# The range checks of four steps, the start of a written row, three routing products and one weight split stand elsewhere

## The chip, the cores and the metric

The kernel runs on one core of one Trainium2 chip. The metric is device time in microseconds: from three runs of the kernel the median counts, and one further run was taken with the hardware profiler. TensorE does the matrix products, VectorE and ScalarE the elementwise work and the copies out of the matmul accumulators, GpSimd some of both, and SP issues most transfers.

## The reference

```python
def reference(**kwargs):
...
    attn_out = _attn_ref(**attn_kwargs)
    B, H, S, D = attn_out.shape
    x = np.ascontiguousarray(attn_out.transpose(0, 2, 1, 3)).reshape(B * S, H * D)
    x = _moe_ref(x=x, **moe_kwargs)
    return _moe2_ref(x=x, **moe2_kwargs)

def _attn_ref(q, k, v, a_re, a_im) -> np.ndarray:
    B, H, S, D = q.shape
    mag = np.sqrt(a_re * a_re + a_im * a_im)
    scale = np.minimum(mag, 0.999) / (mag + 1e-06)
    a_re_n, a_im_n = (a_re * scale, a_im * scale)
...
    for t in range(S):
        ar, ai = (a_re_n[:, :, t, :, None], a_im_n[:, :, t, :, None])
        new_re = ar * S_re - ai * S_im
        new_im = ar * S_im + ai * S_re
        kv = np.einsum('bhd,bhe->bhde', k[:, :, t], v[:, :, t])
        S_re, S_im = (new_re + kv, new_im)
        y[:, :, t] = np.einsum('bhd,bhde->bhe', q[:, :, t], S_re)
...
def _moe_ref(x, w_a, w_b, w_out) -> np.ndarray:
    a = x @ w_a
    b = x @ w_b
    return (a * b @ w_out).astype(np.float32)
...
def _moe2_ref(x, w_skip, w_gate, w1, w2) -> np.ndarray:
...
    do_compute = skip_score > 0
...
    e_idx = np.argmax(logits, axis=1)
...
        h = np.maximum(xc[mask] @ w1[e], 0.0)
        y[mask] = gate_w[mask, None] * (h @ w2[e])
    out[do_compute] = xc + y
    return out.astype(np.float32)
```

B, H, S, D are 4, 8, 768, 48; 3072 tokens of width 384, hidden 1536 in the gated layer, eight experts of hidden 1024. First a recurrence with complex decay, then a dense gated layer, then a layer that sends each token to one of eight experts.

## The kernel before

**Three stages run interleaved.** The recurrence is done in 24 units of 128 tokens (unit u belongs to chunk u div 4, batch u mod 4); two units make a pair. The gated layer is done in 12 groups g of 256 tokens, each fed by one pair, in 12 steps f over the hidden size (`moe1_step`). The expert layer follows at the end; its routing is worked out group by group while the gated layer runs.

**A step of the gated layer.** 18 matmuls (`ab{g}_{f}`, lines 647 to 649) make both hidden products of 128 columns, each weight and input split in a high and a low part. ScalarE copies one half out (`asb`), VectorE multiplies the other half onto it (line 655: the gated product), ScalarE mostly rounds the product (`gh`), VectorE or GpSimd takes the rest (`gl`, line 659), and two steps later six matmuls (`op{g}_0`, `op{g}_1`, lines 631 to 633) add the step to the group's output. Two accumulators serve `ab`, two `op`. The columns of w_gate and w_skip are folded into w_out (ten more columns, `w2s`; line 532 splits them), so a group's output holds the routing logits too. After the last step VectorE copies the logits (`lg`, line 670) and ScalarE the output (`xr`, line 674).

**A unit of the recurrence.** Exponent steps of VectorE and ScalarE (`t1`, `t2`, `lh`, `ll`) make the logs of the decays, two matmuls sum them along the tokens (`l2_{u}`; for the angles `tp_{u}`, fed by `tl` and `th`), sines and cosines turn q and k (`qr`, `kr`), TensorE transposes them, multiplies them in 32-row strips (line 461, into `pcs`), VectorE masks the product (`sc`, line 470), and 64 small matmuls make the output (`y{u}`, line 502) behind 48 that add to the state (`ds{u}`, line 412). `xt` (line 514) brings y into the form that the gated layer reads.

**Range checks.** A fast path is taken only where the decays lie in a range. For units 0 to 5 the test is late: `check_late` loads a_re again into a tile `chk` with one buffer, tests it (`least`, line 285), loads a_im into the same buffer and tests that (`largest`, line 288, into `immax`). The result is needed at the program's end only.

**Routing.** `pick` finds a group's best expert (`m`, `eq`, `rt_oh`, `rt_r`), TensorE counts places (`pp`, lines 735 to 737; while recurrence runs these products use the `pcs` accumulators), `place` makes slots (`sl`, line 789), TensorE makes the table's part (`pt`, line 803), and VectorE adds it to the table (`tbl`, line 804).

**What sets the order.** A scheduler orders each engine's instructions, but `keep_rows` ties some into written rows: `ORDER` for the program's start, `STEADY` for ScalarE and VectorE in the groups in between. In a row `gl{g}_2*3` means three writers of that tile and `:1` the second one; each is made to follow the one before it on its engine, without a wait. `PLACE` lists which of the weight splits and others go to which engine. In `att_trigs`, from a pair on whose first unit is `PORT` = 8 or more, both units' first steps are issued ahead of the rest.

Of the kernel before, what the change touches and what calls it, by code (L numbers as in the profile page):

```python
# [27 lines left out]
NG = 12  # L28
# [3 lines left out]
CAUSAL = 6  # L32
# [25 lines left out]
    "abs": {"scalar": (0, 1, 2, 3,)},  # L58
    "qs": {"gpsimd": (1, 5, 6, 7,)},
    "wh": {"gpsimd": (0, 4, 5,)},  # L60
    "wl": {"vector": (1, 4,)},
    "gl": {"gpsimd": (0, 1, 3, 4, 5, 9, 12, 13, 16, 17, 18, 20, 21,)},
    "add": {"gpsimd": (3,)},
    "magic": {"scalar": (2, 3,)},
# [14 lines left out]
ENGINES = {getattr(mybir.EngineType, x) for x in ("PE", "Activation", "DVE", "Pool")}  # L79
GF = 5  # L80
PORT = 8
ROWS = 64
WO = DM + 10
SKIP_IDX = 8192.0
# [1 line left out]
ORDER = {  # L86
# [5 lines left out]
}  # L92
# [1 line left out]

STEADY = {
    "Activation": "t1_{u}:2 t2_{u}:4 t1_{v}:2 t2_{v}:4 t4_{u}:0 t4_{v}:0 asb{g}_0 th{u} xr{p}*2 gh{g}_0 th{v} asb{g}_1 gh{g}_1 asb{g}_2 gh{g}_2",
    "DVE": "q{u} k{u} q{v} k{v} t4_{u} asb{g}_0 lg{p}*2 tl{u} t4_{v} gl{g}_0 tl{v} asb{g}_1 t3_{u}*2 gl{g}_1 t4_{u} asb{g}_2 qr{u}:1 kr{u}:1 gl{g}_2 t3_{v}*2 qr{u}:0 kr{u}:0 asb{g}_3 t4_{v} gl{g}_3 kr{v}:1 asb{g}_4 kr{v}:0 gl{g}_4 qr{v}:1 qr{v}:0 asb{g}_5 gl{g}_5 sc{u}_0 sc{u}_1 xt{n} asb{g}_6 gl{g}_6 t1_{x} t1_{y} asb{g}_7 t1_{x} ll{x} gl{g}_7 t1_{y} ll{y} asb{g}_8 gl{g}_8 sc{v}_0 sc{v}_1 im{x} imp{x} im{y} imp{y} xt{n} asb{g}_9 gl{g}_9 re{a} re{b} asb{g}_10 gl{g}_10 asb{g}_11 gl{g}_11",
}


def keep_rows(nc, after):

    writers = {}
    for i in nc.all_instructions():
        for o in list(i.outs)[:1]:
            t = getattr(getattr(o, "bass_ap", None), "tensor", None)
            if t is not None:  # L110
                writers.setdefault((i.engine, re.sub(r"_\d+$", "", t.name)), []).append(i)
        if type(i).__name__ == "InstLoadActFuncSet":
            writers.setdefault((i.engine, "tab"), []).append(i)
    for engine, words in ORDER.items():
        chain(writers, after, engine, words.split())
    for engine, words in STEADY.items():
        row = []
        for g in range(3, NG - 1):
            row += words.format(p=g - 1, g=g, n=g + 1, u=2 * g + 2, v=2 * g + 3, x=2 * g + 4, y=2 * g + 5, a=2 * g + 6, b=2 * g + 7).split()
        chain(writers, after, engine, row)  # L120


def chain(writers, after, engine, words):
# [12 lines left out]
def kern(tc, q, k, v, a_re, a_im, w_a, w_b, w_out, w_skip, w_gate, w1, w2, out):  # L136
# [3 lines left out]
    with st:  # L140
# [68 lines left out]
        def after(later, earlier, how=mybir.DependencyClass.NoSync):  # L209
            tc.add_manual_dep(  # L210
                later, earlier.name,
                mybir.DependencyInfo(how, mybir.DependencyReason.DATA),
                reason="table order",
            )
# [72 lines left out]
        def largest(i, im):  # L287
            return dve.tensor_reduce(out=immax[:, i : i + 1], in_=im, axis=AX.X, op=ALU.max, apply_absolute_value=True)

        def check_late(i):  # L290
            c, b = units[i]
            for src, test in ((a_re, least), (a_im, largest)):
                t = ew.tile([P, W], F32, tag="chk", name=f"chk{i}", bufs=1)
                ld = sync.dma_start(t.rearrange("t (h d) -> t h d", d=D), src[b, :, c * P : (c + 1) * P, :].rearrange("h t d -> t h d"))
                after(ld.ins, marks["ts", i + 6])
                test(i, t)

        def att_exp(i):
            c, b = units[i]
# [295 lines left out]
        def att_trigs(p):  # L595
            table("trig_and_small")
            steps = [att_trig(i) for i in (2 * p, 2 * p + 1)]
            if 2 * p >= PORT:
                for x in steps:
                    next(x)  # L600
            for x in steps:
                for _ in x:
                    pass
            if p == 0 and WARM:

                wm = bank("op", "warm", 2)
                for x in range(WARM):
                    pe.matmul(wm[:, :DM], ident, U[0]["ts"], start=True, stop=True)
            for i in (2 * p, 2 * p + 1):
                att_pe(i)  # L610
                if i >= CAUSAL and i % 2 == 0:
                    ready = sorted(picked)
                    for r in sorted(lgs):
                        pick(r, env.masked, env.pc[1])
                elif i > CAUSAL:
                    for r in ready:
                        place(r, env.masked, env.pc[0])
# [21 lines left out]
        def moe1_step(g, f):  # L639
            xt = M[g][0]  # L640
            fs = slice((f % 2) * P, (f % 2 + 1) * P)
            ab = bank("ab", f"ab{g}_{f}", 2)
            for x, nm in enumerate("ab"):
                o = ab[:, x * 256 : (x + 1) * 256]
                for c in range(NCC):
                    wh, wl = (env.w[nm, f // 2][:, y, c, fs] for y in range(2))
                    pe.matmul(o, wl, xt[:, c, 0], start=c == 0, stop=False)  # L647
                    pe.matmul(o, wh, xt[:, c, 1], start=False, stop=False)  # L648
                    pe.matmul(o, wh, xt[:, c, 0], start=False, stop=c == NCC - 1)  # L649
            if len(pend) == 2:  # L650
                moe1_out(*pend.pop(0))
            asb = env.mp.tile([P, 256], F32, tag="asb", name=f"asb{g}_{f}")
            n = NF * g + f
            copy(on("asb", n, act), asb, ab[:, :256])
            dve.tensor_tensor(out=asb, in0=ab[:, 256:], in1=asb, op=ALU.mult)  # L655
            gh = env.mp.tile([P, 256], F32R, tag="gh", name=f"gh{g}_{f}", bufs=3)
            copy(on("gh", n, act), gh, asb)
            gl = env.mp.tile([P, 256], F32R, tag="gl", name=f"gl{g}_{f}", bufs=3)
            on("gl", n).tensor_tensor(out=gl, in0=asb, in1=gh, op=ALU.subtract)  # L659
            pend.append((g, f, gh, gl))  # L660
# [635 lines left out]
```

## Time and profile before

| | us |
|---|---|
| median of 3 runs (832.26 to 834.45) | 832.45 |
| the profiled run | 831.85 |
| its span | 830.0 |
| TensorE busy | 786.5 |
| VectorE busy | 550.4 |
| ScalarE busy | 453.0 |
| GpSimd busy | 167.6 |

The span is what the profile covers; 1.85 us of the run lie outside it. Busy times are sums over the span; an engine with a small sum can still hold TensorE at one place, which only the waits of that place show.

### The profile page before, as it was taken

Reading aid. Unit: us, or ns where it says so; the run is one execution under the profiler, and the core shown is the slowest. Engines: PE = TensorE matmul, PEld = TensorE weight load, DVE = VectorE, ACT = ScalarE, POOL = GpSimd, SP = SyncE. Lnnn points to the kernel's source line nnn. Section 1 sums busy time; section 2 is a strip of 40 time slices with the busy share of each in tenths; the row PEclk is TensorE's granted clock in tenths of the full one; section 3 lists DMA queues with packets and bytes.
Section 4 is the critical chain, followed back from the end, with each engine's and each line's share of the span. In section 5 each row is a group of like instructions: output and inputs, shape, how many; then the busy total and the mean of one; then the engine's idle time right before and its main releaser. Section 6 shows DMA issues by size and latency. Waiting matters only on the chain.

```text
span 830.0 us, 22382 instructions
## 1 busy us (share of the span) xinstructions
PE 786.5 (95%) x9115; PEld 754.2 (91%) x9115; DVE 550.4 (66%) x1417; ACT 453.0 (55%) x949; POOL 167.6 (20%) x196
## 2 busy tenths in 40 slices
PE   1899999999999999999999999999999999999995
PEld 0589899999989989999999999998999989999995
DVE  7999888685676857757676576746747347555541
ACT  6897655473546644566455565555535226555540
POOL 3131443410100000000000000000003026666650
PEclk9999999999999999999999999999999999999998
DMA  9995223251342432213222231120105049667500
GB/s 253 251 316 121 54 63 68 46 122 33 77 89 38 106 64 72 54 36 87 51 68 55 52 81 36 50 49 11 40 18 176 1 164 338 215 222 208 180 22 23
DMA packets 180960, 83.17 MB, mean 100 GB/s; under 512 B 152084, under 2 KB 168026, under 8 KB 180848
## 3 DMA queue, kind: packets, MB, share of 16 engines
q1 hardware_dynamic: 178800, 76.26, 35.7%
q0 software_dynamic: 2048, 5.40, 1.8%
q8 instruction: 73, 1.20, 0.6%
q14 instruction: 39, 0.32, 0.1%
HBM read 69.84 MB, written 12.61 MB: 99 GB/s over the span
## 4 chain that ended last, share of the span: by engine, by line
PE 80%; DVE 6%; DMA 6%; ACT 3%; issue 2%; POOL 1%; SPq 0%; POOLq 0%; DVEq 0%; ACTq 0%
PE ab L647 11%; PE ab L648 10%; PE ab L649 10%; PE op L632 5%; PE op L631 5%; PE op L633 5%; PE y L502 4%; PE eh L954 3%; PE eh L955 3%; PE eh L957 3%; PE eo L971 3%; PE eo L972 3%; PE eo L973 3%; DMA chk<-in_a_im_dram 2%; PE pcs L461 2%
## 5 line engine op out<-in xcount | busy, mean ns | idle before, releaser
L647 PE MATMUL ab<-xt,wa 128*128 128x256 f32 x432 | 124.4, 288 | 0.5 <-DVE asb L655 0.4
L647 PE MATMUL ab<-xt,wb 128*128 128x256 f32 x432 | 123.0, 285 | 0.1
L648 PE MATMUL ab<-xt,wb 128*128 128x256 f32 x432 | 122.5, 284 | 0.0
L649 PE MATMUL ab<-xt,wb 128*128 128x256 f32 x432 | 122.4, 283 | 0.0
L649 PE MATMUL ab<-xt,wa 128*128 128x256 f32 x432 | 121.7, 282 | 0.0
L648 PE MATMUL ab<-xt,wa 128*128 128x256 f32 x432 | 121.6, 281 | 0.0
L659 DVE TENSOR_TENSOR gl<-asb,gh 128x256 fp32r<-128x256 f32 x131 | 62.6, 478 | 64.0 <-ACT gh L279 63.9
L632 PE MATMUL op<-wo,gh 128*128 128x394 f32 x288 | 99.2, 344 | 1.7 <-POOL wo L532 1.7
L633 PE MATMUL op<-wo,gh 128*128 128x394 f32 x288 | 98.7, 343 | 0.0
L631 PE MATMUL op<-wo,gl 128*128 128x394 f32 x288 | 98.5, 346 | 0.0
L279 ACT ACTIVATE asb<-ab 128x256 f32<-128x256 f32 x139 | 52.5, 378 | 68.8 <-PE ab L649 65.2
L647 PEld LDWEIGHTS ab<-xt,wa 128*128 128x128 f32 x432 | 81.4, 188 | 2.4 <-ACT asb L279 0.7
L648 PEld LDWEIGHTS ab<-xt,wb 128*128 128x128 f32 x432 | 81.5, 189 | 1.1 <-issue 1.0
L655 DVE TENSOR_TENSOR asb<-ab,asb 128x256 f32<-128x256 f32 x144 | 60.0, 417 | 33.3 <-ACT asb L279 33.1
L647 PEld LDWEIGHTS ab<-xt,wb 128*128 128x128 f32 x432 | 81.4, 188 | 0.6 <-DVE wb L532 0.3
L649 PEld LDWEIGHTS ab<-xt,wb 128*128 128x128 f32 x432 | 81.3, 188 | 0.7 <-issue 0.6
L648 PEld LDWEIGHTS ab<-xt,wa 128*128 128x128 f32 x432 | 81.4, 188 | 0.5 <-DVE xt L514 0.2
L649 PEld LDWEIGHTS ab<-xt,wa 128*128 128x128 f32 x432 | 81.5, 189 | 0.3 <-issue 0.2
L922 POOL TENSOR_TENSOR wq<-stg,wq 128x768 fp32r<-128x768 f32 x32 | 59.5, 1861 | 95.7 <-DMA stg<-in_moe_w_dram 46.4
L279 ACT ACTIVATE gh<-asb 128x256 fp32r<-128x256 f32 x132 | 54.4, 413 | 36.3 <-DVE asb L655 36.1
L264 POOL MEMSET v<- 128x64 f32 x24 | 3.5, 150 | 339.0 <-PE y L502 246.3
L961 DVE SCALAR_TENSOR_TENSOR hl<-eh,hh 128x256 fp32r<-128x256 f32 x64 | 27.1, 424 | 52.9 <-ACT hh L960 52.8
(268 smaller groups left out, 2021.2 us busy)
## 6 DMA issues: line engine op xcount, KB each, us to landing
stg<-in_moe_w_dram SPq DMA_DIRECT2D x28, 768.0 KB
rawa<-in_moe_w_a_dram SPq DMA_DIRECT2D x6, 768.0 KB
re<-in_a_re_dram SPq DMA_DIRECT2D x24, 192.0 KB
rawb<-in_moe_w_b_dram SPq DMA_DIRECT2D x6, 768.0 KB
q<-in_q_dram SPq DMA_DIRECT2D x24, 192.0 KB
k<-in_k_dram SPq DMA_DIRECT2D x24, 192.0 KB
rawo<-in_moe_w_out_dram SPq DMA_DIRECT2D x6, 768.0 KB
xd<-xr SPq DMA_DIRECT2D x24, 192.0 KB
```

Of the source, the lines that this page charges most:

```text
L279: return act.activation(out=out, in_=in_, func=AF.Copy) if e is act else e.tensor_copy(out, in_)
L502: ins = pe.matmul(o, l[:, col : col + STRIP], r, start=begin, stop=end).ins
L631: pe.matmul(o, gl[:, ts], wh, start=f == 0, stop=False)
L632: pe.matmul(o, gh[:, ts], wl, start=False, stop=False)
L633: i = pe.matmul(o, gh[:, ts], wh, start=False, stop=f == NF - 1)
L647: pe.matmul(o, wl, xt[:, c, 0], start=c == 0, stop=False)
L648: pe.matmul(o, wh, xt[:, c, 1], start=False, stop=False)
L649: pe.matmul(o, wh, xt[:, c, 0], start=False, stop=c == NCC - 1)
L655: dve.tensor_tensor(out=asb, in0=ab[:, 256:], in1=asb, op=ALU.mult)
L659: on("gl", n).tensor_tensor(out=gl, in0=asb, in1=gh, op=ALU.subtract)
L922: lo.tensor_tensor(out=o[:, 1], in0=t, in1=o[:, 0], op=ALU.subtract)
L961: vm = dve.scalar_tensor_tensor(out=gl, in0=o, scalar=0.0, in1=gh, op0=ALU.max, op1=ALU.subtract)
```

## The change

1. `PLACE` gives the small low split of group 3 of w_out to VectorE instead of GpSimd, and VectorE's written start row has it between the two `kr` products of unit 3 (`kr3*2` becomes `kr3 wo3 kr3`).
2. The written rows `STEADY` begin with group 2 instead of 3. In VectorE's row the second unit's exponent step comes ahead of the first unit's `ll`, and the table's sum stands behind the second `xt`.
3. The late checks' tests, kept in a list, are made to follow the gated products of steps 1, 4, 7 and 10 in groups 2, 3 and 4.
4. A row for TensorE in group 11 puts the routing products `pp10`, `pt9` and `pt10` behind whole `ab` blocks.
5. `att_trigs` issues both first steps ahead from pair 3 (`CAUSAL` = 6) instead of pair 4.

```diff
-    "wl": {"vector": (1, 4,)},
+    "wl": {"vector": (1, 3, 4,)},
...
+TESTS = (1, 4, 7, 10)
...
 STEADY = {
...
-asb{g}_7 t1_{x} ll{x} gl{g}_7 t1_{y} ll{y} asb{g}_8
+asb{g}_7 t1_{x} t1_{y} ll{x} gl{g}_7 ll{y} asb{g}_8
...
-im{y} imp{y} xt{n} asb{g}_9
+im{y} imp{y} xt{n} tbl:{r} asb{g}_9
...
+LAST = "ab11_3*18 pp10*3 ab11_4*18 pt9*4 ab11_6*18 pt10*4 ab11_7"
...
-        for g in range(3, NG - 1):
+        for g in range(2, NG - 1):
...
+    chain(writers, after, "PE", LAST.split())
...
+        tests = []
+
         def check_late(i):
...
-                test(i, t)
+                tests.append(test(i, t).ins)
...
-            if 2 * p >= PORT:
+            if 2 * p >= CAUSAL:
                 for x in steps:
                     next(x)
...
-            dve.tensor_tensor(out=asb, in0=ab[:, 256:], in1=asb, op=ALU.mult)
+            i = dve.tensor_tensor(out=asb, in0=ab[:, 256:], in1=asb, op=ALU.mult).ins
+            if g >= 2 and f in TESTS and tests:
+                after(tests.pop(0), i)
```

The diff's two pieces of `STEADY` are cut from VectorE's row. The rows below show how the order of instructions moves; a tile's name ends in its unit or group and a running number, and the lines of the changed kernel are 5 to 9 higher.

VectorE in group 4, around the masked scores of unit 10 and the routing of group 3, before:

```order
L659 TENSOR_TENSOR gl4_5_4630<-asb4_5_4625,gh4_5_4628 128x256
L285 TENSOR_SCALAR chk5_4444,remin_88<-chk5_4444 128x384
L470 TENSOR_TENSOR sc10_0_4171<-pcs0_2188,keep_86 128x512
L470 TENSOR_TENSOR sc10_1_4189<-pcs1_2189,keep_86 128x512
L713 TENSOR_REDUCE m3_4254<-lg3_3958 128x2
L288 TENSOR_REDUCE immax_87<-chk5_4447 128x1
L721 SCALAR_TENSOR_TENSOR eq3_4258<-lg3_3958,m3_4254,desc_117 128x8 x2
L723 TENSOR_TENSOR dl3_4261<-lg3_3958,m3_4254 128x16
L725 TENSOR_REDUCE m23_4263<-eq3_4258 128x2
L728 SCALAR_TENSOR_TENSOR rt_oh_132<-eq3_4258,m23_4263,sk3_4256 128x8 x2
```

The same place after, and the two places where the tests now stand:

```order
L668 TENSOR_TENSOR gl4_5_4630<-asb4_5_4625,gh4_5_4628 128x256
L477 TENSOR_TENSOR sc10_0_4171<-pcs0_2188,keep_86 128x512
L477 TENSOR_TENSOR sc10_1_4189<-pcs1_2189,keep_86 128x512
L722 TENSOR_REDUCE m3_4254<-lg3_3958 128x2
L730 SCALAR_TENSOR_TENSOR eq3_4258<-lg3_3958,m3_4254,desc_117 128x8 x2
...
L662 TENSOR_TENSOR asb4_7_4689<-ab4_7_4664,asb4_7_4689 128x256
L290 TENSOR_SCALAR chk5_4444,remin_88<-chk5_4444 128x384
...
L662 TENSOR_TENSOR asb4_10_4785<-ab4_10_4760,asb4_10_4785 128x256
L293 TENSOR_REDUCE immax_87<-chk5_4447 128x1
```

Both tests of unit 5 left the stretch between `gl4_5` and the routing's one-hot.

TensorE at the start of group 2, around the last `op` of group 1 (`op1`, fed by `gl1_11`), before:

```order
L648 MATMUL ab2_2_2725<-xt2_1657,wb1_491 128x256
L631 MATMUL op1_0_1381<-wo5_1275,gl1_11_2124 128x394
L632 MATMUL op1_0_1381<-wo5_1275,gh1_11_2122 128x394
...
L632 MATMUL op1_1_1382<-wo5_1275,gh1_11_2122 128x394
L633 MATMUL op1_1_1382<-wo5_1275,gh1_11_2122 128x394
L649 MATMUL ab2_2_2725<-xt2_1657,wb1_491 128x256
```

After:

```order
L656 MATMUL ab2_2_2725<-xt2_1657,wb1_491 128x256
L638 MATMUL op1_0_1381<-wo5_1275,gl1_11_2124 128x394
...
L640 MATMUL op1_1_1382<-wo5_1275,gh1_11_2122 128x394
L276 MATMUL tp_6_2288<-tl6_2290,tri_r_74 128x384
L277 MATMUL tp_6_2288<-th6_2289,tri_r_74 128x384
L638 MATMUL op2_0_2671<-wo0_507,gl2_0_2697 128x394
L639 MATMUL op2_0_2671<-wo0_507,gh2_0_2695 128x394
```

Before, the last matmul of `ab2_2` and the 18 of `ab2_3` follow `op1`, `tp_6` was inside `ab2_1` and `op2` came after `ab2_3`; now `tp_6` and `op2` follow `op1` directly.

TensorE and VectorE around the odd unit 13 in group 5, TensorE before and after:

```order
L412 MATMUL ds13_5230<-u13_5152,kr13_4987 32x48 x3
L502 MATMUL y13_5255<-tq13_5154,state1_91 32x128 x4
L648 MATMUL ab5_9_5593<-xt5_4249,wb4_1172 128x256
L649 MATMUL ab5_9_5593<-xt5_4249,wb4_1172 128x256
L647 MATMUL ab5_9_5593<-xt5_4249,wb4_1172 128x256
```

```order
L419 MATMUL ds13_5230<-u13_5152,kr13_4987 32x48 x3
L509 MATMUL y13_5255<-tq13_5154,state1_91 32x128 x4
L509 MATMUL y13_5255<-sc13_0_5210,v13_4051 32x128
L509 MATMUL y13_5255<-tq13_5154,state1_91 32x128
L509 MATMUL y13_5255<-sc13_0_5210,v13_4051 32x128 x2
```

VectorE before and after:

```order
L318 SCALAR_TENSOR_TENSOR t1_14_5712<-t1_14_5712,t2_14_5713 128x384
L327 TENSOR_TENSOR ll14_5726<-t1_14_5712,lh14_5725 128x384
L659 TENSOR_TENSOR gl5_7_5559<-asb5_7_5554,gh5_7_5557 128x256
L318 SCALAR_TENSOR_TENSOR t1_15_5741<-t1_15_5741,t2_15_5742 128x384
L327 TENSOR_TENSOR ll15_5755<-t1_15_5741,lh15_5754 128x384
L655 TENSOR_TENSOR asb5_8_5586<-ab5_8_5561,asb5_8_5586 128x256
L329 TENSOR_TENSOR imp14_4908<-imp14_4908,t2_15_5742 128x384
L659 TENSOR_TENSOR gl5_8_5591<-asb5_8_5586,gh5_8_5589 128x256
L470 TENSOR_TENSOR sc13_0_5210<-pcs0_2188,keep_86 128x512
```

```order
L325 SCALAR_TENSOR_TENSOR t1_14_5712<-t1_14_5712,t2_14_5713 128x384
L325 SCALAR_TENSOR_TENSOR t1_15_5741<-t1_15_5741,t2_15_5742 128x384
L334 TENSOR_TENSOR ll14_5726<-t1_14_5712,lh14_5725 128x384
L668 TENSOR_TENSOR gl5_7_5559<-asb5_7_5554,gh5_7_5557 128x256
L334 TENSOR_TENSOR ll15_5755<-t1_15_5741,lh15_5754 128x384
L662 TENSOR_TENSOR asb5_8_5586<-ab5_8_5561,asb5_8_5586 128x256
L336 TENSOR_TENSOR imp14_4908<-imp14_4908,t2_15_5742 128x384
L668 TENSOR_TENSOR gl5_8_5591<-asb5_8_5586,gh5_8_5589 128x256
L477 TENSOR_TENSOR sc13_0_5210<-pcs0_2188,keep_86 128x512
```

TensorE's whole `y13` (32 entries) now follows `ds13`, where before all but four entries stood behind `ab5_9` and `ab5_10`; on VectorE `t1_15` changed places with `ll14`.

## Rows read from the trace of the kernel before

**Rows 1.** The page: span and busy time of the engines.

```profile
span 830.0 us, 22382 instructions
PE 786.5 (95%) x9115; PEld 754.2 (91%) x9115; DVE 550.4 (66%) x1417; ACT 453.0 (55%) x949; POOL 167.6 (20%) x196
```

**Rows 2.** Windows: us of span; PE busy (instructions), PEld, DVE, ACT, POOL, clock, DMA, GB/s.

```profile
300.00:560.00 260.00, 259.81 (x3615) 250.77 (x3615) 174.81 (x510) 147.79 (x333) 10.37 (x20) 1.00 0.26 57
```

**Rows 3.** Timeline 88 to 92 (start, duration, instruction, [idle before, releaser]); tile wo (min/median/max ns).

```profile
91.41 0.45 PE L632 MATMUL op<-wo,gh 128*128 128x394 f32 x1 [1.67 <-POOL wo L532]
88.12 3.24 POOL L532 TENSOR_TENSOR wo<-w2s,wo 128x20 fp32r<-128x20 f32 x1 [4.22 <-ACT wo L279]
88.52 0.54 DVE L391 TENSOR_TENSOR kr<-k,ts 128x384 f32<-128x384 f32 x1
L532 POOL TENSOR_TENSOR wo<-w2s,wo x4: 230/256/3238, 55.1 to 115.8; 128x20 fp32r<-128x20 f32 x4
L532 DVE TENSOR_TENSOR wo<-w2s,wo x2: 167/167/167, 63.9 to 105.0; 128x20 fp32r<-128x20 f32 x2
```

**Rows 4.** Timeline, group 2, first recurrence unit (6): TensorE, SP's queue, VectorE.

```profile
187.02 0.30 PE L502 MATMUL y<-sc,v 128*32 128x128 f32 x1 [1.58 <-DVE sc L470]
180.99 0.37 SPq L294 DMA_DIRECT2D chk<-in_a_re_dram  x1
184.67 0.55 DVE L285 TENSOR_SCALAR_CACHE_REDUCE chk<-chk 128x384 f32<-128x384 f32 x1 [0.48 <-DMA chk<-in_a_re_dram]
```

**Rows 5.** Timeline, groups 3 and 4, the routing: TensorE and VectorE.

```profile
243.67 0.17 PE L735 MATMUL pcs<-rt_oh,ustrict 128*128 128x16 bf16 x1 [0.81 <-DVE rt_oh L728]
297.06 0.17 PE L735 MATMUL pcs<-rt_oh,ustrict 128*128 128x16 bf16 x1 [2.02 <-DVE rt_oh L728]
295.58 0.55 DVE L288 TENSOR_REDUCE immax<-chk 128x1 f32<-128x384 f32 x1 [1.87 <-DMA chk<-in_a_im_dram]
```

**Rows 6.** Timeline, start of group 5: first and last of six w_out matmuls, then VectorE.

```profile
326.52 0.35 PE L631 MATMUL op<-wo,gl 128*128 128x394 f32 x1
327.44 0.34 PE L633 MATMUL op<-wo,gh 128*128 128x394 f32 x1
327.99 0.54 DVE L362 SCALAR_TENSOR_TENSOR tl<-t,th 128x384 fp32r<-128x384 f32 x1
329.23 0.42 DVE L659 TENSOR_TENSOR gl<-asb,gh 128x256 fp32r<-128x256 f32 x1 [0.15 <-ACT gh L279]
```

**Rows 7.** Timeline, group 5: even unit (12), then odd unit (13).

```profile
344.99 1.29 DVE L470 TENSOR_TENSOR sc<-pcs,keep 128x512 int32<-128x512 int32 x2 [0.67 <-PE pcs L461]
345.27 0.26 PE L412 MATMUL ds<-v,kr 128*32 128x48 f32 x6
346.14 0.28 PE L502 MATMUL y<-sc,v 128*32 128x128 f32 x1
356.49 0.53 ACT L279 ACTIVATE lh<-t 128x384 fp32r<-128x384 f32 x1
357.05 0.56 DVE L327 TENSOR_TENSOR ll<-t,lh 128x384 fp32r<-128x384 f32 x1 [3.00 <-ACT lh L279]
359.41 0.56 DVE L327 TENSOR_TENSOR ll<-t,lh 128x384 fp32r<-128x384 f32 x1 [1.00 <-ACT lh L279]
359.73 0.26 PE L412 MATMUL ds<-v,kr 128*32 128x48 f32 x6
361.13 1.28 DVE L470 TENSOR_TENSOR sc<-pcs,keep 128x512 int32<-128x512 int32 x2
```

**Rows 8.** Timeline, groups 9 and 11: TensorE's last waits, and VectorE's wait ahead of one.

```profile
565.90 0.35 PE L647 MATMUL ab<-xt,wa 128*128 128x256 f32 x1 [0.42 <-DVE asb L655]
571.97 0.25 DVE L804 TENSOR_TENSOR tbl<-tbl,pcs 128x96 f32<-128x96 f32 x1 [1.57 <-PE pcs L803]
572.83 0.42 PE L271 MATMUL l<-ll,tri_r 128*128 128x384 f32 x1 [0.91 <-DVE xt L514]
641.29 0.20 PE L803 MATMUL pt<-rt_r,sl 128*128 128x48 bf16 x1 [1.21 <-DVE sl L789]
```

More of the change, by code (lines that the diff above doesn't have):

```diff
@@ L96 @@
     "Activation": "t1_{u}:2 t2_{u}:4 t1_{v}:2 t2_{v}:4 t4_{u}:0 t4_{v}:0 asb{g}_0 th{u} xr{p}*2 gh{g}_0 th{v} asb{g}_1 gh{g}_1 asb{g}_2 gh{g}_2",
-    "DVE": "q{u} k{u} q{v} k{v} t4_{u} asb{g}_0 lg{p}*2 tl{u} t4_{v} gl{g}_0 tl{v} asb{g}_1 t3_{u}*2 gl{g}_1 t4_{u} asb{g}_2 qr{u}:1 kr{u}:1 gl{g}_2 t3_{v}*2 qr{u}:0 kr{u}:0 asb{g}_3 t4_{v} gl{g}_3 kr{v}:1 asb{g}_4 kr{v}:0 gl{g}_4 qr{v}:1 qr{v}:0 asb{g}_5 gl{g}_5 sc{u}_0 sc{u}_1 xt{n} asb{g}_6 gl{g}_6 t1_{x} t1_{y} asb{g}_7 t1_{x} ll{x} gl{g}_7 t1_{y} ll{y} asb{g}_8 gl{g}_8 sc{v}_0 sc{v}_1 im{x} imp{x} im{y} imp{y} xt{n} asb{g}_9 gl{g}_9 re{a} re{b} asb{g}_10 gl{g}_10 asb{g}_11 gl{g}_11",
+    "DVE": "q{u} k{u} q{v} k{v} t4_{u} asb{g}_0 lg{p}*2 tl{u} t4_{v} gl{g}_0 tl{v} asb{g}_1 t3_{u}*2 gl{g}_1 t4_{u} asb{g}_2 qr{u}:1 kr{u}:1 gl{g}_2 t3_{v}*2 qr{u}:0 kr{u}:0 asb{g}_3 t4_{v} gl{g}_3 kr{v}:1 asb{g}_4 kr{v}:0 gl{g}_4 qr{v}:1 qr{v}:0 asb{g}_5 gl{g}_5 sc{u}_0 sc{u}_1 xt{n} asb{g}_6 gl{g}_6 t1_{x} t1_{y} asb{g}_7 t1_{x} t1_{y} ll{x} gl{g}_7 ll{y} asb{g}_8 gl{g}_8 sc{v}_0 sc{v}_1 im{x} imp{x} im{y} imp{y} xt{n} tbl:{r} asb{g}_9 gl{g}_9 re{a} re{b} asb{g}_10 gl{g}_10 asb{g}_11 gl{g}_11",
 }
+LAST = "ab11_3*18 pp10*3 ab11_4*18 pt9*4 ab11_6*18 pt10*4 ab11_7"
 def keep_rows(nc, after):
@@ L117, in keep_rows @@
         row = []
-        for g in range(3, NG - 1):
-            row += words.format(p=g - 1, g=g, n=g + 1, u=2 * g + 2, v=2 * g + 3, x=2 * g + 4, y=2 * g + 5, a=2 * g + 6, b=2 * g + 7).split()
+        for g in range(2, NG - 1):
+            row += words.format(p=g - 1, r=g - 2 if g > 2 else 9 * NG, g=g, n=g + 1, u=2 * g + 2, v=2 * g + 3, x=2 * g + 4, y=2 * g + 5, a=2 * g + 6, b=2 * g + 7).split()
         chain(writers, after, engine, row)
+    chain(writers, after, "PE", LAST.split())
 def chain(writers, after, engine, words):
```

2 rows, old and new, of the table ORDER are left out of this document.

## Prediction

> **What bounds the kernel now.** I read the page's totals first, then TensorE's busy time in windows, then its waits, then the timeline around each wait. TensorE is busy 786.5 of 830.0 us [rows 1]: the kernel is bound by TensorE, and an edit pays only by what it takes from the 43.5 us in which TensorE stands still. The windows tell where those are not: from 300 to 560 us TensorE is busy 259.81 of 260.00 us at a granted clock of 1.00 [rows 2]. So groups 5 to 8 have nothing to give, and the start (before 60 us) and the routed stage (after 680 us) are not touched by the change. What lies between and can be touched is seven single waits: 1.67 us for a small split of the w_out weights [rows 3], 1.58 us for the masked scores `sc` of unit 6 in group 2 [rows 4], 0.81 and 2.02 us for the routing's one-hot in groups 3 and 4 [rows 5], and 0.42, 0.91 and 1.21 us late in groups 9 and 11 [rows 8]. Behind each stands a VectorE or GpSimd instruction that was late in its own queue.
>
> **The change part by part.** The profiled run is 831.85 us, its span 830.0, and the other 1.85 us lie outside the span; I make the sum against 831.85.
>
> *The small split of group 3 of w_out.* GpSimd's split lasts from 88.12 to 91.36, and TensorE resumes at 91.41 after 1.67 us [rows 3]. The other splits of that form on GpSimd take 0.23 to 0.26, two on VectorE 0.17. On VectorE it stands between two `kr` products; the second began at 88.52, so the split ends near 88.7, a full microsecond before TensorE came to need it (91.41 - 1.67 = 89.74). Gain 1.67; the 0.17 more on VectorE falls on `kr`, whose transpose stands behind this block of `op` in TensorE's order. The row shows a GpSimd instruction that is twelve times as long as its equals while VectorE runs without a pause beside it. The Trainium skill (SBUF — State Buffer, section "Who interferes with whom") says that a VectorE instruction with two SBUF inputs and a GpSimd instruction that reads SBUF exclude each other, whichever issues first holding on; the stretched split agrees with that. By that rule the length is GpSimd's loss of the port and goes away with the move; if it were the cost of this instruction's data, VectorE would pay 3.24 us from 88.5, and the term would be a loss of some 0.4 us. The 0.17 us of VectorE's own splits is the row nearest to the moved one.
>
> *The written row begins with group 2.* TensorE waited 1.58 us for `sc` of unit 6, which VectorE reached late because a range check and the next pair's exponent steps stood ahead of it; the check itself began at 184.67 after 0.48 us for its load [rows 4]. In the changed order no exponent step stands there, unit 0's two checks stand behind the products of steps 3 and 4 and so over a step earlier, and TensorE arrives later besides: 1.58 gained. But the same row takes a cover away. Before, one matmul of ab2_2, then ab2_3, stand between group 1's last `op` and the next `tp`. Now `tp_6` and group 2's first `op` follow group 1's last `op` at once, while VectorE's row demands that group 1's logits be copied before `tl6`, and ScalarE's that `xr1` be copied before `gh2_0`. What this chain lasts is to be read in group 5, which has the same row: the six `op` of a step start from 326.52 to 327.44, 0.18 apart; `tl` ends at 328.53, `gl` at 329.65 [rows 6]. There a step's `ab` matmuls cover it. Without the cover TensorE would wait from 327.62 to about 329.72, less 0.36 us for the two `tp` at the same pace: a new wait of 1.75 us in two pieces. Bounds 1.0 (only the `tl` piece, 328.6 - 327.62) and 2.3 (a further `tl` of 0.54 between). I take 1.75. Group 2 alone thus pays nothing: 1.58 - 1.75.
>
> *The four range checks behind gated products.* In groups 3 and 4 the check of the imaginary part stood between the routing's maximum and its one-hot, and waited for its load (1.87 us in group 4); TensorE's routing product waited 0.81 and 2.02 [rows 5]. Now they stand behind the products of steps 7 and 10, where nothing that TensorE soon needs is queued right behind: `gl` of that step, used two steps later. What follows in the old place is the one-hot itself: without the check it can end 2.3 us earlier in group 4 (1.87, and 0.47 that the check holds VectorE), more than the 2.02; I take group 3 to go the same way. Gain 2.83 in full. Each check costs VectorE 0.55 us as before. The loads share one buffer, so the second load leaves when the first check is done; three steps lie between, against 3.7 us that such a load took (issued 180.99, its check at 184.67) [rows 4]; `ds` of units 12 and 13, three steps apart, lie 14.5 us apart [rows 7]. The loads stand in SP's queue ahead of `re10` and `re11`, needed a group later. The other two checks of group 3 and of group 4, tied to steps 1 and 4, keep the places that they had behind those, with waits on VectorE for which TensorE did not wait before; bounds for what that may do now 0 and 0.55, one check's length, taken as 0.
>
> *Odd units.* With the new row TensorE's `y` of the odd units 9 to 19 follows `ds` at once; before, most of `y` stood behind some 20 `ab` and `op` matmuls. An even unit already runs so: `sc` begins at 344.99, 0.28 us before `ds`, and `y` takes it at 346.14 with no wait. The odd one's `sc` began at 361.13, 1.40 us after `ds` at 359.73 [rows 7]: at that place `y` would wait 1.26 us. Does the row bring `sc` forward? VectorE's `ll15` began only at 359.41, on `lh15`, which ScalarE makes after `t1_15`; and VectorE had put `t1_15` behind `ll14` and its wait of 3.00 us for `lh14` (ScalarE, 356.49). Now `t1_15` comes ahead of `ll14`, and ScalarE makes `lh15` as second instruction after `lh14`, done near 358 at 0.53 apiece; `ll15` runs some 1.4 us sooner, and `sc`, then held by `gl5_8`, begins near 359.9. That is 0.17 after `ds` where the even unit has 0.28 before it, so up to 0.45 late; the even unit's `y` left some of that unused, since `sc`'s first half ended near 345.65 and was taken at 346.14. I take 0.2 for each of the six units: cost 1.2, bounds 0 and 2.7.
>
> *The rest.* In group 9 the gated product ahead of `sc` comes sooner (0.42), and `xt` now goes ahead of the table's sum, which itself waited 1.57 us [rows 8]: 0.25 of the 0.91, since its `y` is not earlier. In group 11 the routing product waits 1.21 us for its slots [rows 8]; two steps further on they are long there: 1.21. The product of group 0 now stands right behind `y6` with two groups' routing in front of it, which for one group takes 1.0 us from the end of the check to the product (296.05 to 297.06) [rows 5]; `y` itself covers most of a second one: cost 0.2, bounds 0 and 1.0.
>
> Sum: 1.67 + 1.58 + 2.83 + 0.42 + 0.25 + 1.21 = 7.96 gained; 1.75 + 1.2 + 0.2 = 3.15 lost; net 4.8 us. From 831.85 that is 827.05, from the median 832.45 it is 827.65; I say 827.3, as if the time before were 832.1.
>
> **The rivals.** *A, the odd units keep their late `sc`.* If ScalarE's row brings nothing forward, each of the six waits 1.26: 7.6 instead of 1.2, and 6.4 more make 833.7, no change. For it: ScalarE's `gh5_8` and `t2_15` are still ahead of `sc`; against it: the order moves exactly the product that held `lh15`. *B, on the other side, the same place worse.* ScalarE's row now puts `asb5_8` behind `lh15`. If `t1_15` comes no sooner than now, `lh15` still ends near 359.4, and `asb5_8`, its product, `gh5_8` and `gl5_8` come one after another behind it, 0.4 to 0.55 each: `sc` near 361.5, 1.77 after `ds`, a wait of 1.64 per unit. Six times that is 9.8 instead of 1.2, 8.6 more: 835.9, slower. From 1.0 us a unit on all gains are gone (6.0 / 6), from 1.5 the kernel is slower. *C, nothing new appears.* If the covers hold in group 2 and the odd units, the gain is 8.0 less 0.2: 824.3. *D, the split and the late waits are gone but come back behind the next instruction:* TensorE arrives 1.67 us earlier at everything that follows in the start, where loads set the pace, and half of the 7.96 is given back: 831.3.
>
> **How the numbers follow.** A measurement can tell about 0.3% from no change, 2.5 us: 829.95 and 834.95 are the limits. My forecast 0.58 (825 to 829.95), C 0.12 (823.5 to 825), D 0.11 (829.95 to 831.5), A 0.11 (831.5 to 834.95), B 0.08. Faster: 0.58 + 0.12 = 0.70. Same: D and A, 0.22. Slower: B, 0.08. The range from 823.5 to 831.5 holds the forecast, C and D, 0.81.
>
> **What would show it.** In the changed profile: no wait on the split near 90 us; two pieces of about 1.0 and 0.75 us on `tl` and `gl` at the start of group 2, and none on `sc` of unit 6; no wait on the one-hot in groups 3 and 4; TensorE without a wait at the odd units' `y`, or with 0.2 us; none on the slots in group 11. Waits of over a microsecond at each odd unit would mean A or B, and a new wait between 92 and 160 us D. The prediction is wrong if group 2's new wait is far from 1.75, or if TensorE's busy time itself moves.

## The result

The changed kernel takes 825.62 us in the median of four runs (825.35 to 825.83), the kernel before 833.16 beside it (832.26 to 834.45): a ratio of 0.9908, with an interval from 0.9891 to 0.9925. It is faster by 7.5 us; 827.3 and a gain of 4.8 were forecast, and the time lies inside the range. The two profiled runs differ by less, 831.85 against 825.83, 6.0 us. Where the rest comes from is told below, with the clock.

The page of the changed kernel, its span and totals:

```profile
span 824.1 us, 22362 instructions
PE 784.9 (95%) x9115; PEld 754.1 (92%) x9115; DVE 549.9 (67%) x1418; ACT 452.4 (55%) x949; POOL 164.0 (20%) x195
```

Against [rows 1] the span is 5.9 us shorter; TensorE's busy time fell by 1.6, its idle time from 43.5 to 39.2. TensorE's waits of the changed kernel (line, what was waited for: us in total, times, longest), with the large ones of the start left out:

```profile
PE op L638 <- DVE gl L668: 1.8, 2, 1.6
PE eh L963 <- DVE hl L970: 1.1, 1, 1.1
PE pg L825 <- DVE rt_r L788: 1.0, 1, 1.0
PE ab L654 <- DVE asb L662: 1.0, 2, 0.7
PE y L509 <- issue: 0.9, 3, 0.4
PE tp L276 <- DVE tl L369: 0.7, 1, 0.7
...
PE l L276 <- DVE xt L521: 0.6, 1, 0.6
```

The split, the scores of unit 6, both one-hots, the slots of group 11 and the 0.42 us of group 9 ([rows 3, 4, 5, 8]) are gone from it, and 0.91 at `l` became 0.6. A wait on a gather in the routed stage, `PE xgp L938 <- DMA xg<-xd,giu: 0.7` before, is gone too; no term stood for it. It goes with the row's start: it is 0.6 to 0.8 in all six kernels here whose written row begins with group 3, and at most 0.2 in the seven whose row begins with group 2; why isn't shown. New are two waits at the start of group 2 and two in group 3. TensorE's timeline there:

```profile
170.11 0.44 PE L276 MATMUL tp<-tl,tri_r 128*128 128x384 f32 x1 [0.72 <-DVE tl L369]
170.97 0.45 PE L638 MATMUL op<-wo,gl 128*128 128x394 f32 x1 [0.24 <-DVE gl L668]
261.53 0.38 PE L654 MATMUL ab<-xt,wa 128*128 128x256 f32 x1 [0.68 <-DVE asb L662]
265.51 0.45 PE L638 MATMUL op<-wo,gl 128*128 128x394 f32 x1 [1.60 <-DVE gl L668]
```

The first two are the pair that was forecast (1.0 and 0.75), at 0.96 us together. The chain behind them, the last `op` on TensorE and the logits, the output and `gl` on VectorE and ScalarE:

```profile
168.88 0.17 DVE L679 COPY lg<-op 128x10 f32<-128x10 f32 x1 [2.90 <-PE op L640]
169.04 0.34 PE L640 MATMUL op<-wo,gh 128*128 128x394 f32 x1
169.09 1.03 ACT L683 ACTIVATE xr<-op 128x384 f32<-128x384 f32 x2 [4.22 <-DVE lg L679]
170.51 0.40 DVE L668 TENSOR_TENSOR gl<-asb,gh 128x256 fp32r<-128x256 f32 x1
```

The last two waits, 2.28 us, no step had. VectorE's timeline in group 3 shows what they hang on:

```profile
260.89 0.25 DVE L813 TENSOR_TENSOR tbl<-tbl,pcs 128x96 f32<-128x96 f32 x1 [2.08 <-PE pcs L812]
261.06 0.42 DVE L662 TENSOR_TENSOR asb<-ab,asb 128x256 f32<-128x256 f32 x1
264.64 0.82 DVE L668 TENSOR_TENSOR gl<-asb,gh 128x256 fp32r<-128x256 f32 x1 [3.16 <-ACT gh L284]
```

In group 3 two groups' tables are summed (groups 0 and 1). The row now puts the second sum ahead of the gated product `asb3_9`, and TensorE makes its input only after `l2` of the next pair. VectorE waits 2.08 us with `asb3_9` behind it; and since `l2` is done by then, ScalarE goes into the next pair's exponents and a load of its function table before it gets to `gh3_9`:

```profile
260.43 1.64 ACT L235 ACTIVATE t<-l 128x384 f32<-128x384 f32 x4 [1.00 <-PE l L277]
262.07 1.28 ACT L208 ACT_TABLE_LOAD   x1
263.37 0.94 ACT L235 ACTIVATE t<-imp 128x384 f32<-128x384 f32 x2
264.21 0.40 ACT L284 ACTIVATE gh<-asb 128x256 fp32r<-128x256 f32 x1
```

At the odd unit 13 TensorE doesn't wait. VectorE and TensorE there, to be read against [rows 7]:

```profile
353.80 0.56 DVE L334 TENSOR_TENSOR ll<-t,lh 128x384 fp32r<-128x384 f32 x1 [1.23 <-ACT lh L284]
354.62 0.56 DVE L334 TENSOR_TENSOR ll<-t,lh 128x384 fp32r<-128x384 f32 x1
356.56 1.28 DVE L477 TENSOR_TENSOR sc<-pcs,keep 128x512 int32<-128x512 int32 x2
```

```profile
356.48 0.26 PE L419 MATMUL ds<-v,kr 128*32 128x48 f32 x6
357.40 0.27 PE L509 MATMUL y<-sc,v 128*32 128x128 f32 x1
```

`sc` begins 0.08 us after `ds`, where it began 1.40 after, and `y` takes it 0.92 after `ds` without a wait. The mechanism is the one that was worked out: `ll15` now follows `ll14` by 0.82 us, where it followed by 2.36.

### The profile page after: what moved, and what is told of

Same layout as the page of the kernel before. It is cut to its first block, busy times and chain, and to the rows that moved or that the text cites. A ratio compares the mean times of both kernels' runs of the same rounds, so it can differ in the third digit from the quotient of the medians.

```text
span 824.1 us, 22362 instructions
## 1 busy us (share of the span) xinstructions
PE 784.9 (95%) x9115; PEld 754.1 (92%) x9115; DVE 549.9 (67%) x1418; ACT 452.4 (55%) x949; POOL 164.0 (20%) x195
## 4 chain that ended last, share of the span: by engine, by line
PE 88%; DVE 4%; DMA 3%; ACT 2%; issue 1%; POOL 1%; SPq 0%; POOLq 0%; DVEq 0%; ACTq 0%
PE ab L654 12%; PE ab L655 12%; PE ab L656 12%; PE op L638 6%; PE op L639 6%; PE op L640 6%; PE y L509 5%; PE eh L963 3%; PE pcs L468 3%; PE eh L964 3%; PE eh L966 3%; PE eo L980 3%; PE eo L981 3%; PE eo L982 3%; DMA stg<-in_moe_w_dram 2%; PE ds L419 1%
```

## The experiments

Theory: the gain is the sum of the waits taken away, less the new ones, and the parts add up. Rivals: the waits come back behind the next instruction; the row from group 2 on takes as much as it gives; TensorE's own time changes with the order. The experiments form three groups (the first four, the next four, the last three), each with its own runs of the kernel before, whose medians are 832.80, 832.53 and 832.74. The changed kernel ran again beside the last group only (825.28); elsewhere "the changed kernel" is the 825.62 above, and a difference of a few tenths between groups says nothing.

**The split alone**, on the kernel before:

```diff
-    "wl": {"vector": (1, 4,)},
+    "wl": {"vector": (1, 3, 4,)},
...
-gl0_7 kr3*2 deca5
+gl0_7 kr3 wo3 kr3 deca5
```

> The kernel before with the weight split of group 3 alone moved to VectorE. Sum of waits: TensorE's 1.67 us near 90 us goes and nothing comes back: 1.7 us faster, and no new TensorE wait from 90 to 160 us. Rival (the start is paced by loads): half of it or more returns as other waits between 92 and 160 us, under 0.8 us faster. Port rival: the split takes 3 us on VectorE too and the wait stays.

831.45 us (829.50 to 832.93, 10 runs) against 832.80; ratio 0.9977 [0.9963, 0.9992], 1.4 us faster with an interval from 0.7 to 3.1. From 60 to 180 us TensorE's waits of over 0.2 us are gone and no other came. By the waits that is the whole term; nothing was given back. On VectorE the split takes 0.17 us (at 88.38), so the port rival's 3 us aren't there. But this run showed something else. TensorE in windows around unit 6's scores, where the old wait, 1.81 us here, still is (after the span: PE busy; the number behind POOL's is the granted clock):

```profile
184.00:186.00 2.00, 0.88 (x21) 0.64 (x21) 2.00 (x7) 0.42 (x1) 0.00 (x0) 1.00 0.77 148
186.00:188.00 2.00, 2.00 (x9) 2.00 (x10) 2.00 (x10) 1.42 (x4) 0.00 (x0) 0.55 0.18 34
188.00:190.00 2.00, 2.00 (x30) 1.74 (x33) 2.00 (x11) 0.37 (x2) 0.00 (x0) 0.60 0.36 72
190.00:192.00 2.00, 2.00 (x31) 1.80 (x24) 1.93 (x10) 0.69 (x2) 0.15 (x1) 1.00 0.10 20
```

Behind the wait the granted clock falls near the lower of its two levels (1.2 instead of 2.4 GHz) for over 3 us. In the profile of the kernel before it doesn't: it is 1.00 throughout from 184 to 192 us.

**The tests alone**, on the kernel before:

```diff
-                test(i, t)
+                tests.append(test(i, t).ins)
...
+            if g >= 2 and f in TESTS and tests:
+                after(tests.pop(0), i)
```

> The kernel before with the late checks' tests alone tied behind the gated products of steps 1, 4, 7 and 10. Sum of waits: the routing's 0.81 and 2.02 us in groups 3 and 4 go, and the 1.58 us of unit 6 in group 2 shrinks by the check's part (0.5 to 1.6): 3.3 to 4.4 us faster. Rival (waits return behind the next instruction): new waits for gated products or gl in groups 2 to 4, under 2 us faster.

827.23 us (826.84 to 827.73) against 832.80; ratio 0.9936 [0.9916, 0.9956], 5.6 us faster. Both waits on the one-hot are gone and 0.8 us stay at unit 6: 3.6 us of waits, which would fit the 3.3 to 4.4 expected, and 2 us beyond it. The four runs lie within 0.9 us; those of the kernel before spread over 4.5. About half of the 2 us goes with the clock: all four runs have a mean granted clock of 0.996 or more, and the eight of the 19 runs before that have it too take 831.8, 4.6 more, as the spans of the two profiles say (830.0 and 825.5).

**The row of group 11 alone**, on the kernel before (the line `LAST` and its chain):

> The kernel before with the written row of group 11 alone. Sum of waits: the 1.21 us for the slots go: 1.2 us faster. If the 0.67 us wait on the gather in the routed stage goes too, it hangs on this row: 1.9 us. Rival: the later table sum delays the routed stage's gathers, no gain.

832.23 us (830.00 to 834.13, 10 runs) against 832.80; ratio 0.9994 [0.9981, 1.0007]. The time doesn't settle it. The profile does: `pt <- sl` with its 1.2 us is no longer among the waits, and the gather's wait stays at 0.8, so it doesn't hang on this row. This profile has the drop of the clock in group 4 (0.50 from 298 to 300 us), behind the old wait on the one-hot, 2.36 us here.

**The old exponent order, with `y` still behind `ds`**, on the changed kernel:

```diff
-asb{g}_7 t1_{x} t1_{y} ll{x} gl{g}_7 ll{y}
+asb{g}_7 t1_{x} ll{x} gl{g}_7 t1_{y} ll{y}
...
+    for g in range(3, 9):
+        n = (12, 11)[g - 3] if g < 5 else 10
+        chain(writers, after, "PE", f"y{2 * g + 3}*32 ab{g}_9:{n}*{18 - n} op{g}_0:21*3 op{g}_1:21*3 ab{g}_10".split())
```

> The changed kernel with the second unit's exponent step back behind the first unit's ll in VectorE's row, and TensorE still made to run y of the odd units 9 to 19 behind ds. If bringing t1 of the second unit forward is what makes the scores ready, each of six odd units now waits 0.8 to 1.6 us: 5 to 9 us slower than the changed kernel, 831 to 835 us. Rival (the scores are early for another reason, the table sum or the checks): no wait, within 0.5 us of the changed kernel.

838.22 us (836.35 to 839.99), 12.6 more than the changed kernel, above the 831 to 835 expected, and slower than the kernel before (1.0060 [1.0037, 1.0084]). TensorE's waits:

```profile
PE y L512 <- DVE sc L480: 5.6, 6, 1.1
...
PE op L641 <- DVE gl L671: 3.2, 3, 2.0
PE ab L657 <- DVE asb L665: 2.6, 5, 1.0
...
PE pk L446 <- DVE kr L401: 1.5, 2, 0.8
```

All six odd units wait, 0.63 to 1.06 us each; other products come late as well, in sum 4.2 us more than in the changed kernel, which neither theory had; VectorE's order changed there too (`state` and `xt` come earlier). So the exponent step's place is what lets `y` follow `ds` at once without a wait. The prediction's rival B, which ended slower, was real in size where `y` is held to that place; with `y` free the old order costs 2.0 us only, as a later experiment shows. The profile holds something else, in windows of the program's start, ahead of every edit's place:

```profile
30.00:40.00 10.00, 7.85 (x124) 6.58 (x123) 9.77 (x16) 7.80 (x13) 2.44 (x2) 0.94 0.85 181
40.00:50.00 10.00, 9.10 (x116) 7.63 (x115) 6.93 (x13) 7.70 (x17) 2.08 (x4) 0.72 1.05 328
```

The granted clock is 0.50 from 40 to 44 us. This run took 839.99; the one with the highest mean clock (0.998) took 836.35, 10.7 above the changed kernel, and the waits listed make 9.8 of that.

**Without the table's word in group 3**, on the changed kernel:

```diff
-r=g - 2 if g > 2 else 9 * NG
+r=g - 2 if g > 3 else 9 * NG
```

> The changed kernel with the word for the table's sum left out of VectorE's row in group 3 only. If the new waits of 0.68 and 1.60 us in group 3 (261.5 and 265.5 us of the changed kernel) come from the gated product and its gl standing behind that sum, which waits 2.08 us for TensorE: both go, 2.3 us faster than the changed kernel, near 823.3 us. Rival (ScalarE's table load and the exponents ahead of gh hold the gl anyway): the 1.60 us stay, under 1 us faster.

823.16 us (821.71 to 824.56), 2.5 us under the changed kernel. Both waits in group 3 are gone; ScalarE's table load alone doesn't hold the `gl`. Without the word (one entry of a written row) the scheduler also moved `l2` of the next pair behind `ab3_11`, so that the exponents come later on ScalarE: the two effects aren't told apart, but the word is the cause of both.

**The three parts without the rows**, on the kernel before (the edits of the first three experiments together; parts 2 and 5 of the change are left out, and part 5 was never run alone):

> The kernel before with the split, the four tests and the row of group 11, but the written rows as before. If these three parts are the whole gain and the row from group 2 on gives back what it takes: 824 to 825.5 us, as fast as the changed kernel or faster, with a wait of 0.8 us left at unit 6. Rival (the row's y directly behind ds saves TensorE time): 1 to 2 us slower than the changed kernel, 826.5 to 827.5.

824.19 us (823.90 to 824.62) against 832.53; ratio 0.9891 [0.9864, 0.9919]. It is 1.1 to 1.4 us under the changed kernel's two medians, but its span, 822.9, is no shorter than the 822.8 of that kernel's second profile (824.1 in the first). The wait at unit 6 is 0.9, and `y` of the odd units is split as before. The row from group 2 on, with its new words and with part 5, thus gave nothing in sum; that it took back more than it gave isn't certain.

**Cover at the start of group 2, and no table word**, on the changed kernel:

```diff
+    gl = writers[(mybir.EngineType.DVE, "gl1_11")][0]
+    for i in writers[(mybir.EngineType.DVE, "immax")]:
...
+            after(i, gl)
+    chain(writers, after, "PE", "ab2_1*18 op1_0:33*3 op1_1:33*3 ab2_2*18 tp_6*2".split())
...
-r=g - 2 if g > 2 else 9 * NG
+r=g - 2 if g > 3 else 9 * NG
```

(The lines left out pick the tests of units 10 and 11.)

> The changed kernel without the table's word in group 3, and at the start of group 2 with the last op of group 1 ahead of ab2_2 and the angle tests of units 10 and 11 behind gl1_11, so that ab2_2 covers the logits' copies. If the new wait there (0.72 + 0.24 us) is want of cover: it goes too, 3.2 us faster than the changed kernel, near 822.4 us. Rival: gl1_11 is itself late and TensorE waits for it instead, as fast as without this edit (823.3) or slower.

821.44 us (821.14 to 822.63) against 832.53; ratio 0.9858 [0.9831, 0.9886]. This beats the changed kernel by 4.2 us and the kernel before by 11.1. TensorE in windows, with nothing idle at either place:

```profile
160.00:180.00 20.00, 20.00 (x173) 19.66 (x172) 14.31 (x36) 12.16 (x28) 6.13 (x6) 1.00 0.43 102
250.00:290.00 40.00, 40.00 (x615) 38.76 (x606) 30.98 (x99) 20.34 (x46) 2.28 (x3) 1.00 0.36 80
```

The same windows of the changed kernel:

```profile
160.00:180.00 20.00, 19.03 (x161) 18.09 (x159) 13.43 (x34) 10.44 (x25) 4.85 (x6) 1.00 0.36 89
250.00:290.00 40.00, 37.72 (x460) 36.15 (x463) 28.50 (x89) 21.28 (x48) 1.82 (x3) 1.00 0.36 77
```

**The row from group 3 as before**, on the changed kernel:

```diff
-        for g in range(2, NG - 1):
+        for g in range(3, NG - 1):
```

> The changed kernel with the written rows beginning with group 3 as before, all else kept. If group 2's part takes 0.96 us by the new wait and gives 0.8 (what the tests alone leave at unit 6): the same as the changed kernel within 0.5 us, with the two waits at the start of group 2 gone and one of about 0.8 us back at unit 6. Rival (the row in group 2 is what frees unit 6 altogether): the whole 1.58 us comes back there, 0.6 us slower.

826.07 us (825.28 to 826.10), 0.45 above the changed kernel and, by the two profiles' spans (823.6 and 824.1), 0.5 below: no difference. The pair at the start of group 2 is gone, and 0.8 us are back at unit 6, as expected; the gather's wait is back too, at 0.6. Group 2 in the row is worth nothing by itself.

**Unit 5's tests back, one edit**, on the changed kernel; TensorE's order is the same but for the order inside `y`:

```diff
-                after(tests.pop(0), i)
+                t = tests.pop(0)
+                if g < 4:
+                    after(t, i)
```

> The changed kernel with the two tests of unit 5 alone back where they were, around the scores of unit 10 in group 4; TensorE's order is the same. By the sum of waits TensorE waits 2.0 us again for the one-hot and the kernel is 2.0 us slower than the changed one, every run alike. If such a wait also costs clock: some runs show a stretch behind it at a lower granted clock and are another 1 to 2 us longer, the median 2.5 to 4 us slower, and runs spread over more than 1.5 us where those of the changed kernel lie within 0.5.

829.41 us (827.13 to 830.41, 6 runs) where the changed kernel took 825.28 beside it: 4.1 us for a wait of 2.1. TensorE's timeline at the wait, and windows behind it:

```profile
296.28 0.17 PE L746 MATMUL pcs<-rt_oh,ustrict 128*128 128x16 bf16 x1 [2.14 <-DVE rt_oh L739]
```

```profile
294.00:296.00 2.00, 0.14 (x5) 0.10 (x1) 1.17 (x6) 0.26 (x2) 0.15 (x1) 1.00 0.43 85
296.00:298.00 2.00, 1.72 (x10) 1.72 (x10) 2.00 (x13) 0.72 (x2) 0.00 (x0) 0.60 0.27 46
298.00:300.00 2.00, 2.00 (x9) 2.00 (x8) 1.52 (x5) 0.51 (x2) 0.00 (x0) 0.54 0.00 0
300.00:302.00 2.00, 2.00 (x18) 1.85 (x16) 0.34 (x1) 0.60 (x2) 0.00 (x0) 1.00 0.00 0
```

Two microseconds with next to no work on TensorE, then 4 us at 0.60 and 0.54: some 1.7 us lost, an estimate from these two windows (2 x 0.40 + 2 x 0.46). One of the six runs had a mean clock of 0.997 and took 827.13; the changed kernel's six runs of 0.996 or more have a median of 825.4, 1.7 less. The other five had 0.994 or 0.995 and took 827.6 to 830.4. So the wait costs about its own time, and the drop of the clock on top in most runs.

**The old exponent order, `y` left to the scheduler**, on the changed kernel (the first two lines of the fourth experiment's diff alone):

> The changed kernel with the second unit's exponent step back behind the first unit's ll, and TensorE's order left to the scheduler, which splits y of the odd units 9 to 19 around ab and op again. If y in one piece saves TensorE time: TensorE busy 1 to 1.6 us longer, 1.2 us slower than the changed kernel, no waits at y. Rival (the change from ab to y and back is free): the same as the changed kernel within 0.5 us.

827.25 us (825.18 to 828.70), 2.0 above the changed kernel's 825.28 beside it, with overlapping runs, where 1.2 was expected. The profile carries the reading: from the start of `ds` to the second block of `op` behind it, the same matmuls in both (one `ab` more here at unit 9), the six odd units take 42.9 us in the changed kernel and 44.0 here. At unit 15, the changed kernel first:

```profile
407.79 0.26 PE L419 MATMUL ds<-v,kr 128*32 128x48 f32 x6
414.94 0.34 PE L638 MATMUL op<-wo,gl 128*128 128x394 f32 x1
```

```profile
408.44 0.26 PE L419 MATMUL ds<-v,kr 128*32 128x48 f32 x6
415.87 0.35 PE L638 MATMUL op<-wo,gl 128*128 128x394 f32 x1
```

In sum that is 1.1 us with `y` in one piece, unevenly: 0.06 to 0.54 us at five of the units, while unit 11 is 0.18 slower. That the saved time is TensorE's change between shapes isn't shown. The rest of the 2.0 isn't accounted for.

**The changed kernel again:**

> The changed kernel itself beside the other two on one chip: 825.6 us within 0.5, runs within 1 us of each other; a wait of 0.7 and 0.2 us at the start of group 2 and of 0.7 and 1.6 in group 3 as in its first profile.

825.28 us (824.05 to 827.58), with the four new waits as before (0.7 at `tp`, 0.9 and 1.9 in sum at `ab` and `op`). The runs lie 3.5 us apart, not 1: two of them, 825.99 and 827.58, show a mean clock of 0.995 and 0.992. The changed kernel isn't free of the drop. Where it falls in those runs isn't known, since the profiled one has none; the 1.60 us in group 3 and the program's start, where the fourth experiment's profile has one, are left as candidates.

## Why the prediction was right, and where its terms were off

- **The split, 1.67: right.** The wait is gone in every kernel that has the edit, and nothing came back by 160 us (rival D fell).
- **The tests, 2.83, and unit 6, 1.58: right in waits, short in time.** The waits went as forecast, most of it by the tests: they alone take 3.6 of the 4.4 us, the row the other 0.8. What the sum lacked is the clock behind such waits. Of the 37 runs of the kernel before beside the experiments, 18 have a mean clock of 0.996 or more and a median of 831.7 us, and 19 have less and a median of 833.3. The profiled run that the sum was made on is one of the first kind (0.997), the median of all lies between. Of the changed kernel's runs 6 of 8 are of the first kind. Runs of the first kind alone give 831.7 against some 825.4: 6.3 us, close to the profiles' 6.0; about 1 us of the 7.5 goes with the rarer drop.
- **The start of group 2, -1.75: right in place and mechanism, too large.** It measured 0.96. The step took the chain from group 5, where VectorE was in two range checks until 327.91 and `lg` and `xr` began after all six `op`; here both engines stood waiting, and the first half's copies ran while `op1_1` was still being made. From the start of the last `op` at 169.04 it is 1.47 us to `gl`, instead of 1.79 [rows 6].
- **The odd units, -1.2: mis-sized, wrong in sign.** `sc` came to 0.08 us after `ds`, as worked out within 0.1, and `y` found it in time: cost 0, where 0.2 a unit was taken. On the other side, `y` in one piece saved some 1.1 us over the six units and had no term.
- **The table's sum, +0.25: right in group 9 (0.3), and a term of -2.28 missing in group 3.** The working looked at the sum in the group where it had been late, not in the one group where two sums fall together. Behind a wait in a written row everything in that row waits; of this one only the next `xt` had been asked after.
- **Group 11, 1.21, and group 0's product, -0.2: 1.2 and 0.**

By profile: 8.0 of waits gone as forecast, 0.7 at the gather and 1.1 at the odd units on top, 0.96 and 2.28 new, some 0.7 in small waits at `ab` in group 11 and at `y`: 5.9 us, the spans' difference, of which 1.6 show as less busy time on TensorE and 4.3 as less idle time. The three costs were taken 2.2 us too high (0.8 at group 2, 1.2 at the odd units, 0.2 at group 0's product), the 2.28 of group 3 had no term, and neither had the gains at the gather and in `y`. These nearly cancelled, so the number came out better than its parts, and that part of it is luck.

The prediction named two signs of its own being wrong. The first came: group 2's new wait is 0.96, about half of 1.75. The second isn't clear: TensorE's busy time fell by 1.6 us, but the changed kernel's own two profiles differ by 1.8 in it (784.9 and 783.1). The mechanisms held, of the waits taken away and of the cover lost; the list of what the new row makes wait was not complete.

## What to carry to other kernels

An instruction that a word puts into a fixed order holds up everything behind it when it has to wait. So ask of each word, in every iteration and above all in the irregular ones, what it waits for: here group 3 lost 2.3 us by a word that was harmless in seven others. An edit that removes a stall of some 2 us from a busy TensorE can be worth more than the stall where the clock drops behind it (a wait of 2.1 us, put back, cost 4.1), and a wide spread of the runs is a hint of it. Price a new wait from a place where the engines stand as idle as they will.

## What the runs showed of the hardware

In three profiles TensorE's granted clock was near the lower of its two levels for 3 to 4 us behind a single wait in otherwise unbroken matmul work: behind 1.81 us for the scores of unit 6 (0.55 and 0.60 from 186 to 190 us, the split alone), behind 2.14 us at group 4's one-hot (0.60 and 0.54 from 296 to 300, unit 5's tests back) and behind 2.36 us there (0.50 from 298 to 300, the row of group 11 alone). It stayed at 1.00 behind 1.58 and 2.02 us at the same two places in the profile of the kernel before, and behind 2.22 us at the one-hot in that of the split alone. One more drop stands where no edit reaches, in the start of the fourth experiment's profile (0.50 from 40 to 44 us, behind two waits of 0.73 and 0.74).

Over all runs whose clock is on record, the mean clock is under 0.996 in 40 of the 63 runs of the four kernels that keep the one-hot's wait of 2.0 to 2.4 us, and in 6 of the 36 of the eight that don't. So the drop comes more often with such a wait, but not in every execution and not only there; where a run without a profile has it isn't known. Where it came in group 4 with unit 5's tests back, it cost some 1.7 us, by the estimate above.
